# Attention ahead of two expert layers: 14 pieces of small diagonal tiles in place of 48 groups

## The chip, the cores and the metric

The kernel runs on one core of a Trainium2 chip. The metric is the time of one execution on the device in microseconds, median of three runs: 916.33 us (914.98 to 916.78) before. Of the core's engines, PE (TensorE) does matmuls and transposes and has a queue of its own for loading weights (PEld), DVE (VectorE) and POOL (GpSimd) do elementwise work and reductions, ACT (ScalarE) does functions and copies, SP issues the DMAs.

## The reference

q, k, v have shape (4 batches, 8 heads, 576 positions, 64). Heads 0 to 3 look back over a window of 32 positions, heads 4 to 7 at all earlier positions that lie a multiple of 32 back:

```python
scores = scale * np.matmul(q, k.transpose(0, 1, 3, 2))
rel = pos[:, None] - pos[None, :]
mask_local = (rel >= 0) & (rel < stride)                       # stride = 32
mask_strided = (rel >= 0) & (pos[None, :] % stride == pos[:, None] % stride)
scores = np.where(mask, scores, -1000000000.0)
attn = np.exp(scores - max); attn = attn / (sum + 1e-09)
x = attn @ v                                                   # -> x [2304, 512]
h = np.maximum(x @ w_in, 0.0);  x = h * h @ w_out              # d_ff 2048
h = x @ w_in2;  P = a0 + a1*h + a2*h**2 + a3*h**3
Q = 1 + abs(b0)*abs(h) + abs(b1)*h**2
out = (P / (Q + 1e-6)) @ w_out2
```

Everything is fp32; the weights reach the kernel as 64-bit doubles.

## The kernel before, in words

**Tokens and units.** The 2304 tokens are cut into 6 blocks of 384 (`NB`, `TB`), d_ff into 16 parts of 128 (`NF`). Step (j, f) of the first layer does `h_unit` (L473): 128 hidden rows for block j, 12 matmuls 128x384, since each fp32 product is made of three fp32r products (high by high, low by high, high by low). Two steps later `o_unit1` (L513) adds the squared, split hidden rows into four accumulators, 12 matmuls again. The second layer has the same `h_unit` and an `o_unit2` (L676) of nine matmuls 128x512. A "unit" is one of these: 384 in all. They run in order of j and f, block 0 first, and block j needs all heads of its 384 rows of `x`.

**Weights.** A half (`wraw`, 512 KB) comes from DRAM as int64, `to_f32` turns it into floats with one ACT operation (L210) and three DVE passes (L211, L212, L213), and `split_w` makes the high and low parts on POOL (L229, L230; the low part of the first four on DVE). The 32 halves of the first layer are converted by `feed_w` in the head and in block 0, two a step; those of the second layer in blocks 1 to 4, and go to a scratch in DRAM (`spill_w`). In block 0 the subtraction `gl` (L491) of the hidden rows' low part is on DVE too.

**Attention.** It is cut into 48 groups of one batch, one pair of heads and one third: a local group has two tiles of 96 queries by 128 keys for each head, a strided one all queries and keys of 14, 14 or 4 residue classes modulo 32, as tiles of 126x126 (seven classes of 18 positions) or 72x72 (four). Two groups share their loads and their scores: the two halves of the array's rows hold their 64-deep products. The mask is a matmul of an identity with a constant (L297) ahead of the scores (L305); from group 24 on it is added by DVE (L314). Then for each group: maximum (L317) and its product with -1/8 (L318) on DVE, one exponential on ACT for each tile and head with its sum read out behind it (L334), sum and reciprocal on DVE (L344, L345), product on POOL (L347), transposes on PE (L354), their copy out of PSUM (L360, L362), values on PE (L370), and `at_out`: the high part of `x` by ACT (L395), the low part by DVE (L396).

**Order.** Ahead of block 0 a loop over slots runs the groups that block 0 needs. The others are a list of pieces (a pair's scores with its softmax, or one group's values with another's transposes), and `paces` says how many of them must have been issued by each step; they stand ahead of the step's `h_unit`. PSUM has seven banks for everything ("ps") and one for weight bits.

The lines of the kernel before that the diff touches, and what calls them:

Of the kernel before, what the change touches and what calls it, by code (L numbers as in the profile page):

```python
# [9 lines left out]
F32 = mybir.dt.float32  # L10
# [8 lines left out]
P = 128  # L19
# [5 lines left out]
TB = 384  # L25
# [4 lines left out]
QL, KL = 96, 128  # L30
RG = ((0, 7), (14, 7), (28, 4))
MASKED = -8.0e9
C_L0, C_L1, C_S7, C_S4, C_ID, C_END = 0, 128, 256, 382, 454, 582


def _constants():

    c = np.zeros((P, C_END), np.float32)
    r, k = np.arange(QL)[:, None], np.arange(KL)[None, :]
    for at, rel in ((C_L0, r - k), (C_L1, r + STRIDE - k)):  # L40
        c[:QL, at : at + KL] = np.where((rel >= 0) & (rel < STRIDE), 0.0, MASKED)
# [8 lines left out]
class Group:


    def __init__(self, b, hp, i):
        self.b, self.hp, self.i = b, hp, i
        self.local = hp < NPAIR // 2
        if self.local:
            self.nt, self.nq, self.nk = 2, QL, KL
        else:  # L60
            self.r0, self.nr = RG[i]
            self.nt = 2 if self.nr == 7 else 1
            self.nq = self.nk = self.nr * NA
        self.name = f"{b}_{hp}_{i}"

    def q_positions(self):
        if self.local:
            return np.stack([np.arange(QL) + QL * (2 * self.i + t) for t in range(2)])
        a, r = np.arange(NA)[:, None], np.arange(self.nr)[None, :]
        return np.stack([(a * STRIDE + r + self.r0 + t * self.nr).ravel() for t in range(self.nt)])  # L70

    def k_positions(self):
        if self.local:
            return np.stack([np.arange(KL) + max(0, QL * (2 * self.i + t) - STRIDE) for t in range(2)])
        return self.q_positions()

    def k_starts(self):
        if self.local:
            return (0, 64) if self.i == 0 else (0, 96)
        return tuple(t * self.nk for t in range(self.nt))  # L80

    @property
    def qn(self):
        return self.nt * self.nq

    @property
    def kn(self):
        return 224 if self.local else self.qn

    def pieces(self):  # L90


        if self.local:
            t0 = self.b * S + 2 * QL * self.i
            return [(t0 // TB, t0 % TB, None)]
        out = []
        a = 0
        while a < NA:
            t0 = self.b * S + a * STRIDE
            n = min(NA - a, (TB - t0 % TB) // STRIDE)  # L100
            out.append((t0 // TB, t0 % TB, (a, n)))
            a += n
        return out


def _groups():

    out = []
    for b in range(B):
        strided = [Group(b, hp, i) for i in ((2, 0, 1) if b == 0 else range(3)) for hp in (2, 3)]  # L110
        local = {i: [Group(b, hp, i) for hp in (0, 1)] for i in range(3)}
        early = local[0] + local[1]
        out += early + strided + local[2] if b == 2 else strided + early + local[2]
    return out


def _last_group(groups):

    last = [0] * NB
    for n, g in enumerate(groups):  # L120
        for j, _, _ in g.pieces():
            last[j] = max(last[j], n)
    return last


QK_W = 1008
V_W = 2 * 2 * D


def _pack_qkv(q, k, v):  # L130

    groups = _groups()
    qk = np.zeros((len(groups), D, QK_W), np.float32)
    vp = np.zeros((len(groups) // 2, P, 2, V_W), np.float32)
    for n, g in enumerate(groups):
        h = slice(2 * g.hp, 2 * g.hp + 2)
        qpos = g.q_positions().ravel()
        if g.local:
            k0 = int(g.k_positions()[0, 0])
            kpos = np.arange(k0, k0 + g.kn) if k0 + g.kn <= S else np.arange(k0, S)  # L140
        else:
            kpos = qpos
        qk[n, :, : 2 * g.qn] = q[g.b, h][:, qpos].transpose(2, 0, 1).reshape(D, -1)
        kt = qk[n, :, 2 * g.qn : 2 * (g.qn + g.kn)].reshape(D, 2, g.kn)
        kt[:, :, : len(kpos)] = k[g.b, h][:, kpos].transpose(2, 0, 1)
        vt = v[g.b, h][:, g.k_positions()]
        vp[n // 2, : g.nk, n % 2, : g.nt * 2 * D] = vt.transpose(2, 1, 0, 3).reshape(g.nk, -1)
    return qk.reshape(len(groups) // 2, P, QK_W), vp.reshape(len(groups) // 2, P, 2 * V_W)
# [8 lines left out]
def moe_kernel(ctx, tc, qk, vp, w1, w2, a, b, masks, eye, out):  # L157
    nc = tc.nc
    groups = _groups()
    last = _last_group(groups)  # L160
    NG = len(groups)
# [17 lines left out]
    sms = [cpool.tile([P, 28], F32, name=f"sm{i}") for i in range(6)]  # L179
# [61 lines left out]
    st = {}  # L241
    loaded = [0]
    FIRST, PLACES, LATE, WARM = 12, 8, 24, 10

    def lags(n):

        return (3, 4) if n < FIRST else (2, 3)

    def load_qk(p):

        n = 2 * p
        if n >= NG:
            return
        g = groups[n]
        if n < FIRST:
            t = wpool.tile([P, QK_W], F32, tag=f"wh{NF - 1 - p}", name=f"qk{g.name}")
        else:
            t = apool.tile([P, QK_W], F32, tag="qk", name=f"qk{g.name}")
        w = 2 * (g.qn + g.kn)
        nc.sync.dma_start(t[:, :w], qk[p][:, :w])  # L260
        for m in range(2):
            st[n + m] = dict(qk=t[m * D : (m + 1) * D])

    def load_v(p):
        n = 2 * p
        if n >= NG:
            return
        g = groups[n]
        if n < FIRST:
            vt = wpool.tile([P, 2, 2, 2, D], F32, tag=f"w{'hl'[p % 2]}{7 - p // 2}", name=f"v{g.name}")  # L270
        else:
            vt = apool.tile([P, 2, 2, 2, D], F32, tag="v", name=f"v{g.name}")
        nc.sync.dma_start(vt, vp[p].rearrange("p (m t h d) -> p m t h d", m=2, h=2, d=D))
        for m in range(2):
            st[n + m]["v"] = vt[:, m]

# [491 lines left out]
```

## Time and profile before

| | us |
|---|---|
| median of three runs | 916.33 (914.98 to 916.78) |
| profiled execution, span | 912.5 |
| PE busy | 892.7 (98%) |
| DVE busy | 637.8 (70%) |
| POOL busy | 552.1 (61%) |
| ACT busy | 542.1 (59%) |

The span runs from the first to the last instruction of the profiled execution; the measured times also hold what lies around it, so the span stands 3.8 us below the median. Busy time is the time in which an engine has an instruction in work; PE's overlap in its pipeline, so that the durations of single matmuls in the timeline are longer than the distance from one start to the next. Small fp32 matmuls appear as two records each.

### The profile page before, as it was taken

What the parts mean: (1) busy time and instruction counts of PE and PEld (TensorE: products, weight loads), DVE (VectorE), ACT (ScalarE), POOL (GpSimd) and SP (SyncE); (2) the same over time, 40 slices, a digit from 0 to 9 for tenths busy, and PEclk for the clock granted to TensorE, in tenths of its full rate; (3) what the DMA queues carried; (4) which work ended last, traced back from release to release, by engine and by line L of the source; (5) the groups of instructions that cost most, each with busy time, mean ns of one, the idle gap of its engine ahead of it and who ended that gap; (6) DMA issues with size and microseconds to landing.
All of it is one profiled execution on the core that took longest, in us unless ns stands there. A gap on an engine that the chain in (4) does not pass through costs nothing.

```text
span 912.5 us, 14815 instructions
## 1 busy us (share of the span) xinstructions
PE 892.7 (98%) x5232; PEld 822.0 (90%) x5232; DVE 637.8 (70%) x888; ACT 542.1 (59%) x1384; POOL 552.1 (61%) x567
## 2 busy tenths in 40 slices
PE   7799899999999999999999999999999999999998
PEld 5589799998998999999999999989999999999896
DVE  5999865656465565554213598888888888888885
ACT  6777654445445554433325677776777767776763
POOL 2478755444454544544233496877787787777674
PEclk8899999999999999999999999999999999999999
DMA  8873445535544533532475710100100100100000
GB/s 325 284 233 122 124 132 159 167 111 169 174 138 141 181 129 118 167 109 77 162 263 214 250 38 1 54 18 1 52 18 1 53 18 1 44 1 1 36 0 35
DMA packets 40106, 98.56 MB, mean 108 GB/s; under 512 B 4704, under 2 KB 11616, under 8 KB 40032
## 3 DMA queue, kind: packets, MB, share of 16 engines
q1 hardware_dynamic: 40032, 97.62, 32.2%
q8 instruction: 41, 0.67, 0.3%
q14 instruction: 33, 0.27, 0.1%
HBM read 71.39 MB, written 26.21 MB: 107 GB/s over the span
## 4 chain that ended last, share of the span: by engine, by line
PE 84%; ACT 2%; DVE 1%; DMA 0%; issue 0%; POOL 0%; SPq 0%; ACTq 0%; POOLq 0%
PE h L473 40%; PE acc L676 22%; PE acc L513 18%; PE ps_t L354 1%; PE ps_v L370 1%; PE ps_s L305 1%; ACT e L334 1%; DMA x_scratch<-x 0%; DVE w L213 0%; DVE r L487 0%; DVE w L212 0%; DVE w L211 0%; ACT w L210 0%; ACT r L483 0%; POOL spl L230 0%
## 5 line engine op out<-in xcount | busy, mean ns | idle before, releaser
L473 PE MATMUL h<-xh,wh 128*128 128x384 f32 x768 | 263.2, 343 | 0.6 <-ACT e L334 0.6
L473 PE MATMUL h<-xh,wl 128*128 128x384 f32 x768 | 258.3, 336 | 0.0
L473 PE MATMUL h<-xl,wh 128*128 128x384 f32 x768 | 257.8, 336 | 0.0
L645 DVE RECIPROCAL h<-w 128x384 f32<-128x384 f32 x96 | 245.1, 2553 | 0.7 <-POOL w L642 0.7
L641 POOL TENSOR_TENSOR p<-p,hs 128x384 f32<-128x384 f32 x96 | 98.8, 1029 | 111.3 <-ACT p L639 111.3
L473 PEld LDWEIGHTS h<-xh,wh 128*128 128x128 f32 x768 | 144.7, 188 | 8.0 <-ACT e L334 1.8
L473 PEld LDWEIGHTS h<-xl,wh 128*128 128x128 f32 x768 | 144.8, 188 | 3.9
L473 PEld LDWEIGHTS h<-xh,wl 128*128 128x128 f32 x768 | 144.4, 188 | 0.0
L513 PE MATMUL acc<-gh,wh 128*128 128x384 f32 x384 | 129.0, 336 | 0.0
L513 PE MATMUL acc<-gh,wl 128*128 128x384 f32 x384 | 128.7, 335 | 0.0
L513 PE MATMUL acc<-gl,wh 128*128 128x384 f32 x384 | 128.6, 335 | 0.0
L491 POOL TENSOR_TENSOR gl<-r,gh 128x384 fp32r<-128x384 f32 x75 | 78.2, 1044 | 81.7 <-ACT gh L490 79.4
L483 ACT ACTIVATE r<-h 128x384 f32<-128x384 f32 x91 | 44.8, 492 | 119.7 <-PE h L473 113.0
L676 PE MATMUL acc<-wh,gl 128*128 128x512 f32 x288 | 113.9, 395 | 0.0
L676 PE MATMUL acc<-wl,gh 128*128 128x512 f32 x288 | 113.7, 395 | 0.0
L487 DVE TENSOR_TENSOR r<-r 128x384 f32<-128x384 f32 x75 | 55.9, 745 | 82.0 <-ACT r L483 81.6
L636 ACT ACTIVATE sq<-h 128x384 f32<-128x384 f32 x96 | 47.6, 496 | 110.0 <-PE h L473 106.5
L676 PE MATMUL acc<-wh,gh 128*128 128x512 f32 x288 | 111.9, 389 | 0.0
L643 DVE SCALAR_TENSOR_TENSOR p<-p,co,h 128x384 f32<-128x384 f32 x96 | 58.7, 612 | 65.6 <-POOL p L641 65.5
L662 POOL TENSOR_TENSOR gl<-rq,gh 128x384 fp32r<-128x384 f32 x96 | 99.1, 1033 | 2.0 <-ACT gh L661 2.0
L642 POOL TENSOR_TENSOR w<-w,sq 128x384 f32<-128x384 f32 x96 | 98.7, 1028 | 0.0
L490 ACT CAST gh<-r 128x384 fp32r<-128x384 f32 x91 | 47.1, 517 | 59.9 <-DVE r L487 59.5
(81 smaller groups left out, 1563.1 us busy)
## 6 DMA issues: line engine op xcount, KB each, us to landing
wraw<-in_w SPq DMA_DIRECT2D x64, 512.0 KB, 4.3
w_scratch<-sph SPq DMA_DIRECT2D x32, 256.0 KB, 4.2
w_scratch<-spl SPq DMA_DIRECT2D x32, 256.0 KB, 3.4
wh<-w_scratch SPq DMA_DIRECT2D x16, 512.0 KB, 3.6
wl<-w_scratch SPq DMA_DIRECT2D x16, 512.0 KB, 4.5
v<-in_vp SPq DMA_DIRECT2D x24, 256.0 KB, 3.9
qk<-in_qk SPq DMA_DIRECT2D x12, 416.0 KB, 3.8
x_scratch<-x SPq DMA_DIRECT2D x24, 192.0 KB, 2.5
```

Of the source, the lines that this page charges most:

```text
L473: nc.tensor.matmul(ps[:, :TB], w[:, c], x[:, kk, :], start=(kk == 0 and i == 0), stop=(kk == KT - 1 and i == 2))
L487: nc.vector.tensor_tensor(h, h, h, ALU.mult)
L490: last_act = nc.scalar.copy(gh, h).ins
L491: low = lambda: (nc.vector if psum_h or j == 0 else nc.gpsimd).tensor_tensor(gl, h, gh.bitcast(F32), ALU.subtract)
L513: nc.tensor.matmul(acc[j][e][:, :TB], w[:, c], g, start=(f == 0 and i == 0), stop=(f == NF - 1 and i == 2))
L636: keep(nc.scalar.activation(sq, h, AF.Square))
L641: keep(nc.gpsimd.tensor_tensor(p1, p1, hs, ALU.mult))
L642: keep(nc.gpsimd.tensor_tensor(w, w, sq, ALU.add))
L643: keep(nc.vector.scalar_tensor_tensor(p1, p1, a1, h, ALU.add, ALU.mult))
L645: keep(nc.vector.reciprocal(h, w))
L662: keep(nc.gpsimd.tensor_tensor(gl, rq, gh.bitcast(F32), ALU.subtract))
L676: nc.tensor.matmul(p, g[:, t * P : (t + 1) * P], w[:, c], start=(f == 0 and i == 0), stop=(f == NF - 1 and i == 2))
```

## The change

The 48 groups become 14 pieces. A strided piece is one batch and one pair of heads: 11 slots of three residue classes, each a tile of 54 queries by 54 keys (six slots in the upper half of the array's columns or rows, five in the lower, which overlap in one class). A local piece is one token block with all four local heads: 12 runs of 32 queries, each with the 64 keys that end with it. A piece's scores fill two PSUM banks, one for each head of the pair(s), 128 rows by 324 or 384 columns. Softmax is one chain a bank: maximum, subtraction into SBUF, one exponential of the whole bank on ACT, sum, 1e-9, reciprocal and POOL's product; then three 128x128 transposes, one copy, and values of 54 or 32 columns.

Of instructions, a strided piece has 24 score matmuls (64 deep, 64 rows, 54 columns), 6 transposes and 22 value matmuls, a local one 48 (64 deep, 32 rows, 64 columns), 6 and 48 (32 columns). Its loads are 585 KB and 384 KB, or 2 x 400 KB and 2 x 384 KB. Three pieces stand ahead of block 0; `PLAN` names the step of each other: scores and softmax ahead of that step's unit, both banks' transposes two steps on, values three steps on. The mask is a matmul up to piece 5 and a DVE addition from piece 6 on. The low part of all weights is on POOL, and the first eight weight halves are loaded right behind the loads of the head.

```diff
+    ORDER = [("s", 0, 2), ("s", 0, 3), ("l", 0), ("l", 1), ("s", 1, 2), ("s", 1, 3), ("l", 2), ("l", 3),
+             ("s", 2, 2), ("s", 2, 3), ("l", 4), ("s", 3, 2), ("s", 3, 3), ("l", 5)]
+    HEAD, MASK_PE = 3, 6
...
+    def at_scores(p):
+        for r in range(2):
+            p.ps[r] = psum.tile([P, 512], F32, tag="ps", name=f"ps_s{p.name}_{r}")
+        late = p.n >= MASK_PE
...
+            if not late:
+                pin(p, nc.tensor.matmul(to, cst[:, C_ID : C_ID + P], mask, start=True, stop=False, skip_group_check=True))
...
+        def score(r, at, col, lhs, rhs):
+            m = lhs.shape[1]
+            pin(p, nc.tensor.matmul(
+                p.ps[r][at : at + m, col * p.w : (col + 1) * p.w], lhs, rhs, start=late, stop=True, skip_group_check=True))
+
+        if p.strided:
+            t = p.qk[0]
+            for m in range(3):
+                for i in range(2):
+                    for s in range(2):
+                        u = min(2 * m + s, S_SLOTS[i][1] - 1)
+                        q0, k0 = (6 * i + u) * W3, QS_W + (S_SLOTS[i][0] + 3 * u) * NA
+                        for r in range(2):
+                            rows = slice(r * D, (r + 1) * D)
+                            score(r, s * 64, 2 * m + i, t[rows, q0 : q0 + 64], t[rows, k0 : k0 + W3])
+            return
+        for m in range(3):
+            for hp in range(2):
+                for c in range(4):
+                    j = 4 * m + c
+                    k0 = QL_W + _local_window(p.at, j)
+                    for r in range(2):
+                        x = p.qk[hp][r * D : (r + 1) * D]
+                        score(r, c * STRIDE, 2 * m + hp, x[:, j * STRIDE : (j + 1) * STRIDE], x[:, k0 : k0 + EW])
+
+    def at_softmax(p, r):
...
+        if p.n >= MASK_PE:
+            nc.vector.tensor_tensor(to, to, mask, ALU.add)
+        nc.vector.tensor_reduce(sm[:, 0:6], s3, AX.X, ALU.max)
...
+        nc.vector.tensor_tensor(ev, s3, wide(0), ALU.subtract)
+        nc.scalar.activation(ev, ev, AF.Exp, scale=1.0 / 8.0)
+        nc.vector.tensor_reduce(sm[:, 6:12], ev, AX.X, ALU.add)
+        nc.vector.tensor_scalar(sm[:, 12:18], sm[:, 6:12], 1e-9, None, ALU.add)
+        nc.vector.reciprocal(sm[:, 18:24], sm[:, 12:18])
+        nc.gpsimd.tensor_tensor(ev, ev, wide(18), ALU.mult)
...
+        for m in range(3):
+            src = p.e[r][:, 2 * m : 2 * m + 2, :].rearrange("p a k -> p (a k)")
+            pin(p, nc.tensor.transpose(ps[:, m * P : (m + 1) * P], src, ident))
...
+        nc.scalar.copy(p.t[r], ps[:, : 3 * P])
...
+        for j in range(12):
+            for i in range(2):
+                rows = slice(i * 64, (i + 1) * 64)
+                for r in range(2):
+                    value(i, r, j * STRIDE, STRIDE, p.t[r][rows, j * STRIDE : (j + 1) * STRIDE], p.v[r][rows, j, :])
...
-    while slot < last[0] + 5:
-        at_slot(slot)
...
+    at_scores(P0)
+    warm_up(2)
+    at_softmax(P0, 0)
+    at_softmax(P0, 1)
+    at_scores(P1)
+    at_softmax(P1, 0)
+    at_transpose(P0, 0)
+    at_softmax(P1, 1)
+    at_transpose(P0, 1)
+    at_scores(P2)
+    at_softmax(P2, 0)
+    at_values(P0)
+    at_softmax(P2, 1)
...
+    PLAN = {3: (0, 0), 4: (0, 5), 5: (0, 10), 6: (1, 1), 7: (1, 7), 8: (2, 0), 9: (2, 5), 10: (2, 10), 11: (3, 0), 12: (3, 5), 13: (3, 10)}
...
+        for step, do in ((0, sc), (2, tr_both), (3, va)):
+            at_unit.setdefault((j, f + step), []).append((do, pieces[n]))
```

On DVE, around the first two `gl` subtractions of block 0, before: `gl_0_0` and `gl_0_1` are those of the first two steps, L211 to L213 the three passes of a weight conversion, L317 a softmax maximum.

```order
L212 SCALAR_TENSOR_TENSOR bits_1_597<-wraw_1_1_302,bits_1_597 128x512
L491 TENSOR_TENSOR gl_0_0_633<-r_0_629,gh_0_0_632 128x384
L213 SCALAR_TENSOR_TENSOR wraw_1_1_302<-wraw_1_1_302,bits_1_597 128x512
L211 TENSOR_SCALAR bits_0_609<-w_0_4_0_608 128x512
L212 SCALAR_TENSOR_TENSOR bits_0_609<-wraw_4_0_370,bits_0_609 128x512
L491 TENSOR_TENSOR gl_0_1_689<-r_1_685,gh_0_1_688 128x384
L213 SCALAR_TENSOR_TENSOR wraw_4_0_370<-wraw_4_0_370,bits_0_609 128x512
L317 TENSOR_REDUCE sm_81<-ps_s_2_1_691 126x4
```

The same place after; the conversion's passes are L162 to L164 there, `gl` is L401, and L298, L308, L310 to L312 are the softmax of the local piece of block 1 (`sl`, `el`).

```order
L164 SCALAR_TENSOR_TENSOR wraw_2_0_119<-wraw_2_0_119,bits_0_480 128x512
L401 TENSOR_TENSOR gl_0_0_596<-r_0_592,gh_0_0_595 128x384
L401 TENSOR_TENSOR gl_0_1_638<-r_1_634,gh_0_1_637 128x384
L298 TENSOR_REDUCE sm_81<-ps_sl_0_487 128x6
L298 TENSOR_REDUCE sm_82<-ps_sl_1_488 128x6
L308 TENSOR_TENSOR el_0_540<-ps_sl_0_487,sm_81 128x384
L308 TENSOR_TENSOR el_1_548<-ps_sl_1_488,sm_82 128x384
L310 TENSOR_REDUCE sm_81<-el_0_540 128x6
L310 TENSOR_REDUCE sm_82<-el_1_548 128x6
L311 TENSOR_SCALAR sm_81<-sm_81 128x6
L162 TENSOR_SCALAR bits_1_560<-w_0_0_1_559 128x512
L312 RECIPROCAL sm_81<-sm_81 128x6
```

Before, conversions stand between the two subtractions and ahead of the next softmax; after, the subtractions and nearly the whole softmax of two banks stand ahead of the fourth conversion's first pass.

On PE, ahead of a step of block 2, before: values of one group and transposes of the next lie between an `acc` unit and an `h` unit.

```order
L513 MATMUL acc_2_3_2683<-gh_2_4_2780,wh_4_606 128x384
L513 MATMUL acc_2_3_2683<-gl_2_4_2781,wh_4_606 128x384
L513 MATMUL acc_2_3_2683<-gh_2_4_2780,wl_4_607 128x384
L370 MATMUL ps_v_2_1_2912<-at_2_1_2756,v_2_1_2567 64x126 x4
L354 MATMUL ps_t_3_1_2917<-ident,e_3_1_2637 126x126 x4
L473 MATMUL h_2_7_2928<-xh_2_797,wh_7_814 128x384
L473 MATMUL h_2_7_2928<-xl_2_798,wh_7_814 128x384
```

The same kind of place after, at step 2 of block 2: both banks of one piece are transposed, two steps behind its scores.

```order
L423 MATMUL acc_1_3_1810<-gh_1_15_2511,wh_15_1415 128x384
L423 MATMUL acc_1_3_1810<-gl_1_15_2512,wh_15_1415 128x384
L423 MATMUL acc_1_3_1810<-gh_1_15_2511,wl_15_1416 128x384
L320 MATMUL ps_ts_2_0_2664<-ident,es_2_0_2555 128x128 x3
L320 MATMUL ps_ts_2_1_2670<-ident,es_2_1_2565 128x128 x3
L383 MATMUL h_2_2_2676<-xh_2_1124,wh_2_477 128x384
L383 MATMUL h_2_2_2676<-xl_2_1125,wh_2_477 128x384
```

Values and transposes no longer share a visit; a visit holds the transposes of a whole piece.

## Rows read from the trace of the kernel before

**Rows 1.** The page: span, and each engine's busy time.
```profile
span 912.5 us, 14815 instructions
...
PE 892.7 (98%) x5232; PEld 822.0 (90%) x5232; DVE 637.8 (70%) x888; ACT 542.1 (59%) x1384; POOL 552.1 (61%) x567
```

**Rows 2.** The chain of waits: start us, us, what; one unit each.
```profile
348.46 2.08 PE acc L513 x12
...
525.98 2.08 PE acc L676 x9
```

**Rows 3.** Timeline of PE: start us, us, operation; first scores, two blocks' first, last matmul.
```profile
4.40 0.76 PE L305 MATMUL ps_s<-qk 64*72 64x72 f32 x8
...
41.61 0.42 PE L473 MATMUL h<-xh,wh 128*128 128x384 f32 x1
...
126.91 0.44 PE L473 MATMUL h<-xh,wh 128*128 128x384 f32 x1
...
908.34 0.39 PE L676 MATMUL acc<-wh,gl 128*128 128x512 f32 x1
```

**Rows 4.** Windows, head and block 0: length, PE, PEld, DVE, ACT, POOL busy, clock, DMA, GB/s.
```profile
0.00:41.60 41.60, 30.71 (x250) 20.50 (x251) 29.40 (x93) 27.54 (x130) 14.66 (x33) 0.84 0.88 317
41.60:126.90 85.30, 81.30 (x541) 74.30 (x539) 77.97 (x151) 55.84 (x162) 65.32 (x66) 0.98 0.52 164
```

**Rows 5.** Windows of the tiles ps_s, ps_t, ps_v: length, PE, PEld, DVE, ACT busy.
```profile
126.90:440.00 313.10, 12.34 (x178) 9.92 (x176) 27.83 (x50) 34.28 (x192) 1.00 0.43 138
...
126.90:440.00 313.10, 14.71 (x100) 9.39 (x100) 0.00 (x0) 13.17 (x27) 1.00 0.43 138
...
126.90:440.00 313.10, 15.42 (x208) 9.91 (x208) 11.70 (x40) 11.04 (x40) 1.00 0.43 138
```

**Rows 6.** Timeline of PE, block 3: two visits of the attention between units.
```profile
345.05 1.12 PE L305 MATMUL ps_s<-qk 64*96 64x128 f32 x16
346.09 0.44 PE L473 MATMUL h<-xh,wh 128*128 128x384 f32 x1
...
350.48 0.55 PE L370 MATMUL ps_v<-at,v 128*64 128x96 f32 x8
350.96 0.55 PE L354 MATMUL ps_t<-ident,e 96*128 96x96 f32 x4
351.29 0.42 PE L473 MATMUL h<-xh,wh 128*128 128x384 f32 x1
351.55 0.33 PE L473 MATMUL h<-xl,wh 128*128 128x384 f32 x1
```

**Rows 7.** Timeline of PE, block 0: small matmuls of 126 and 72 columns.
```profile
59.32 0.65 PE L370 MATMUL ps_v<-at,v 126*64 126x126 f32 x8
59.90 0.65 PE L354 MATMUL ps_t<-ident,e 126*126 126x126 f32 x4
60.31 0.42 PE L513 MATMUL acc<-gh,wh 128*128 128x384 f32 x1
...
64.78 0.48 PE L305 MATMUL ps_s<-qk 64*72 64x72 f32 x8
65.19 0.44 PE L473 MATMUL h<-xh,wh 128*128 128x384 f32 x1
```

**Rows 8.** Groups of instructions by shape: count, busy us, mean ns, idle before.
```profile
L211 DVE TENSOR_SCALAR bits<-w 128x512 int32<-128x512 int32 x32 | 22.0, 687 | 0.4 <-ACT w L210 0.2
L491 DVE TENSOR_TENSOR gl<-r,gh 128x384 fp32r<-128x384 f32 x16 | 15.0, 935 | 4.4 <-ACT gh L490 4.4
L347 POOL TENSOR_TENSOR e<-e,sm 126x504 f32<-126x504 f32 x12 | 12.4, 1030 | 17.5 <-DVE sm L345 17.5
L317 DVE TENSOR_REDUCE sm<-ps_s 126x4 f32<-126x504 f32 x16 | 10.3, 671 | 0.0
L396 DVE TENSOR_TENSOR xl<-ps_v,xh 128x192 fp32r<-128x192 f32 x24 | 8.4, 351 | 9.4 <-ACT xh L395 9.4
L318 DVE TENSOR_REDUCE sm<-sm 96x4 f32<-96x8 f32 x24 | 3.4, 149 | 0.0
```

More of the change, by code (lines that the diff above doesn't have):

```diff
@@ L47, in _constants @@
     c[:, C_ID : C_ID + P] = np.eye(P)
     return c.astype(mybir.dt.np(BF16)), np.eye(P, dtype=np.float32)
[L52 to L103, printed above, removed]
@@ L106, in _groups @@
-def _groups():
-    out = []
-    for b in range(B):
[L110 to L123, printed above, removed]
@@ L126 @@
[L126 to L148, printed above, removed]
+W3 = 54
@@ L378, in at_out @@
-    def at_out(n):
-        g, s = groups[n], st.pop(n)
-        ps = s["o"]
-        for j, t0, ar in g.pieces():
-            xh, xl = x_block(j)
-            if g.local:
-                views = [z[:, g.hp, t0 : t0 + 2 * QL] for z in (xh, xl)]
-                src = ps[:, : 2 * QL]
-            else:
-                a0, na = ar
+        for hp in range(2):
+            if p.n < HEAD:
+                t = wpool.tile([P, QKL_W], F32, tag=("wh7", "wl7")[hp], name=f"qk{p.name}_{hp}")
+            else:
+                t = apool.tile([P, QKL_W], F32, tag="qk", name=f"qk{p.name}_{hp}")
+            nc.sync.dma_start(t, ql[p.at, hp])
+            p.qk.append(t)
@@ new lines, in at_values, with value @@
+    def at_values(p):
+        p.o = [psum.tile([P, 512], F32, tag="ps", name=f"ps_v{p.name}_{i}") for i in range(2)]
+        def value(i, r, col, w, at, v):
+            pin(p, nc.tensor.matmul(
+                p.o[i][r * D : (r + 1) * D, col : col + w], v, at, start=True, stop=True, skip_group_check=True))
+        if p.strided:
+            for u in range(6):
+                for i in range(2):
+                    if u < S_SLOTS[i][1]:
+                        rows = slice(i * 64, i * 64 + W3)
+                        c0 = (u // 2) * P + (u % 2) * 64
+                        for r in range(2):
+                            value(i, r, u * W3, W3, p.t[r][rows, c0 : c0 + W3], p.v[0][rows, r, u, :])
+            return
+        for j in range(12):
+            for i in range(2):
+                rows = slice(i * 64, (i + 1) * 64)
+                for r in range(2):
+                    value(i, r, j * STRIDE, STRIDE, p.t[r][rows, j * STRIDE : (j + 1) * STRIDE], p.v[r][rows, j, :])
@@ new lines, in split_x, with at_out @@
+    def split_x(dst, src):
+        nc.scalar.copy(dst[0], src)
+        nc.vector.tensor_tensor(dst[1], src, dst[0].bitcast(F32), ALU.subtract)
+    def at_out(p):
+        if not p.strided:
+            x = x_block(p.at)
+            for hp in range(2):
+                split_x([z[:, hp, :] for z in x], p.o[hp][:, :TB])
+            return
+        a0 = 0
+        while a0 < NA:
+            t0 = p.at * S + a0 * STRIDE
+            na = min(NA - a0, (TB - t0 % TB) // STRIDE)
+            x = x_block(t0 // TB)
+            for i, (base, nu) in enumerate(S_SLOTS):
@@ L568, in load_raw @@
             place, free = homes[k]
-            if slot < free or place and any(homes[i][0] == place for i in range(done, k)):
+            if phase < free or place and any(homes[i][0] == place for i in range(done, k)):
                 break
@@ L708, in moe_kernel @@
         block0[0] = j == 0
[L709 to L714 removed]
+        for do, p in at_unit.get((j, f), ()):
+            do(p)
         while lows:
```

400 lines of the change are left out of this document (170 added, 230 removed).

## The prediction, made before the run

> **What bounds the kernel now.** I read the page first. TensorE (PE) is busy 892.7 of 912.5 us [rows 1], so time can only come from what PE does or from the few places where it stands still. The chain of waits says what its normal work costs: a unit, twelve 128x384 matmuls of `h` or `acc` or nine 128x512 ones of the second layer, takes 2.08 us wherever nothing else is mixed in [rows 2]. There are 6 blocks x 16 steps x 4 products = 384 units, 798.7 us, which this change leaves alone. So 912.5 - 798.7 = 113.8 us is all that it can touch.
>
> The timeline of PE says where those lie. The first `h` starts at 41.61, that of block 1 at 126.91, the last matmul at 908.34 [rows 3]; 4.1 us follow it. Block 0 holds 16 `h` and 14 `acc` units (62.4 us) in its 85.3 us: 22.9 us are over. From 126.91 on, 384 - 30 = 354 units are left, 736.3 us of 781.4; 45.1 us are over. Head 41.6, block 0 22.9, stream 45.1, tail 4.1: together 113.7.
>
> The windows tell head and block 0 apart [rows 4]. In the head PE is busy 30.7 of 41.6 us with the softmax chains of some ten groups between its bursts. In block 0 VectorE (DVE) is the fuller engine against what it has to do: 77.97 of 85.30, with weight conversion, the `gl` subtractions and softmax. Later PE runs without gaps, and the attention costs what its bursts add to PE.
>
> **Part 1, the head.** Before, the first block of `h` waits for ten groups; now for three pieces (`s0_2`, `s0_3`, `l0`). Scores of before started at 4.40 on a load of 144 KB, 128 x 288 floats [rows 3]. The first load is now 585 KB and stands with a 142 KB mask ahead of the first softmax; 583 KB more at the 317 GB/s of the head [rows 4] is 1.9 us, so I put the first score at about 6.3 and the first bank at 6.6. All loads of the head, 3.8 MB, need 12 us at that rate: the first weights land near 16, ahead of their turn on DVE.
>
> Then DVE's order decides, since it has to pass these before `x` of block 0 is whole: three wide passes (maximum, subtraction, sum) for each of six banks. A wide pass over 126x504 takes 0.671 us [rows 8], so 0.43 for 324 columns and 0.51 for 384: 4 banks x 3 x 0.43 + 2 x 3 x 0.51 = 8.2. Twelve small ones at the 0.149 of the 4-column reduction [rows 8]: 1.8. `xl` at 0.351 for 192 columns [rows 8]: 594 columns for each strided piece, 768 for the local one, 1956 in all: 3.6. Two weight conversions of three passes of 0.687 [rows 8]: 4.1. The sum is 17.7, and 6.6 + 17.7 = 24.3. Instructions start a little before the one ahead has ended, which takes perhaps 1 off; exponentials, POOL products and transposes that DVE waits for put 1 to 6 on. I take first `h` at 25, with 22 to 31 as its ends.
>
> **Part 2, block 0.** An earlier start is not all kept, because the conversions were spread over head and block 0 and now nearly all fall into block 0. DVE has from the third to the 29th conversion, 27 x 2.06 = 55.6; 14 `gl` subtractions x 0.935 = 13.1 [rows 8]; the local piece `l1` 6 x 0.51 + 4 x 0.15 + 1.4 = 5.1; two strided pieces 2 x (6 x 0.43 + 0.6 + 1.1) = 8.6: together 82.4. PE has 62.4 of units and some 9 of attention, 71.5, so DVE binds. The two fences of the change show an early loss: DVE now comes to two `gl` and both softmax banks of `l1` before conversion four goes on, and the transposes of `l1` stand in PE's order ahead of the third `h`. For that idle time of DVE, and for the split on POOL behind the last conversion, I add 4.6. Block 0 takes 87, 25 + 87 = 112 for `h` of block 1 (107 to 118), against 126.91: 15 us gained.
>
> **Part 3, the stream.** Before, from 126.9 on the attention's bursts are busy 12.34, 14.71 and 15.42 us, 42.5 together [rows 5]. They lie in 40 visits between units. A burst's busy time runs some 0.08 beyond where the next starts (345.05 + 1.12 against 346.09; 350.48 + 0.55 against 350.96; at a transpose 0.22), and the first `h` behind it starts 0.1 slower than its fellows [rows 6]. So about 0.1 of each visit is counted twice, and 42.5 - 4 = 38.5 is what goes.
>
> After it come eight pieces (four strided, four local), each with three visits. The prices: four pairs of values took 0.58 at 126 columns, four pairs of scores 0.41 at 72 [rows 7], that is 0.17 / 4 / 54 = 0.79 ns a column and pair, and 0.18 for the start. A pair at 54 columns is then 0.045, at 64 0.052, at 32 0.027. Two records make one fp32 matmul; the two row or column halves run as a pair. Transposes: four in 0.41 [rows 7], so six 0.65, with their start 0.86. Three visits start for 0.3 each, 0.9.
> How many small tiles run beside each other, four or eight, is shown by no row, so I bound it.
> - From below, all that differ in place run together. Strided: 12 x 0.045 + 11 x 0.045 = 1.0; local: 12 x 0.052 + 24 x 0.027 = 1.3. With 1.76 for the rest, 4 x (2.8 + 3.1) = 24.
> - Two at a time, as in the rows: strided 24 x 0.045 + 22 x 0.045 = 2.1; local 48 x 0.052 + 48 x 0.027 = 3.8. 4 x (3.9 + 5.6) = 38.
> - None beside another: twice that without the rest, 4 x (5.9 + 9.4) = 61.
>
> I take 31, midway between the first two, since the nearest rows show pairs and nothing shows a limit at two. So the stream changes by 31 - 38.5 = -7.5.
> The Trainium skill, "TensorE: Matmul & The Clock Gate", section "Wait — 56ns, not 53.3ns?", says that matmuls never start closer than about 25 ns apart however few columns they have. By that, an estimate from its figure: 4 x (92 + 192) x 0.025 + 14 = 42 in place of 31, and a time about 11 us later. No row here goes below it: 72 columns have (0.41 - 0.18) / 8 = 28 ns a record [rows 7]. It is rival 1 below, with the row's own figure.
>
> **Part 4, a wait that is added.** Transposes of both banks stand two units of work (8.3 us of PE) behind their scores. What has to fit: add, maximum, subtraction, sum on DVE for two banks, 8 x 0.5 = 4, exponentials, one POOL product a bank (1.03 at 504 columns [rows 8], so 0.7 to 0.8), and a conversion of 2.06 that may stand between on DVE. That is 6 to 9 us. Behind a transpose that waits, PE's `h` and all of the following stand still. Nine to eleven pieces times 0 to 1 us: I take 2 in the stream (0 to 8).
> Costs that I put at nothing: the mask add of late pieces (two of some 0.5 on DVE, which is busy 78 us of 85 only in block 0; late pieces come after it), ACT's one exponential in place of four, POOL's memsets, the loads of later pieces, issued a whole piece ahead of their use. If DVE's cover goes, they count as part of the 8.
>
> **Sum.** 112 + 781.4 - 7.5 + 2 = 887.9 for the last matmul, against 908.34; with the 4.1 of the tail a span of 892. The profiled execution's span, 912.5, lies 3.8 us below the median of 916.33, which I add: 896.
>
> **Rivals.**
> 1. *The number of small matmuls binds.* A record costs 28 ns however many run beside each other: strided 92 x 0.028 = 2.6, local 192 x 0.028 = 5.4, with 1.76 each 4 x (4.3 + 7.1) = 46, 15 more than taken, and 2 in head and block 0: 913. For it: nothing in the trace is faster per record. Against it: what limits the pairs there is their columns, since the price goes with them.
> 2. *The head's gain is lost in block 0.* PE waits at each of the three pieces for the softmax that stands behind conversions on DVE (rows of DVE's order), 3 x 3 us more, and the head ends near 27: `h` of block 1 at 121, 905. For it: DVE is 77.97 of 85.30 full already [rows 4]. Against it: fewer groups are left to do there.
> 3. *Slower: small tiles run one after another.* If a change of place in the array drains what is in flight, the stream's bursts cost 61 in place of 31, and head and block 0 lose 6: 932. It decides from A = 51 on, where the gain of the other parts is used up. For it: nothing shows more than two beside each other; against it: the pairs do overlap, 0.58 for eight at 126 columns, which is 0.07 a record [rows 7], when one alone by the same 0.79 ns would be 0.1.
> The Trainium skill, "TensorEngine Tiling (Array Packing)", section "Instruction Overhead", speaks for the dearer end too: each matmul has some 60 cycles of overhead, one column costs as much as sixty, and a dimension that is already small should not be tiled. An estimate by it: local values at 32 columns would cost like 60, about 1 us more for each local piece, 900 in all.
>
> **How the numbers follow.** Forecast 896 with 0.60: its own range is 884 to 906 (head and block 0 from 107 to 118, bursts from 24 to 38). Rival 1 0.15, rival 2 0.16, rival 3 0.09. The range for 8 in 10 reaches over rivals 1 and 2: 882 to 917; left out are rival 3, the far side of rival 1 and a little below. This kernel's runs differ by 0.2% (914.98 to 916.78 around 916.33), so less than that is no change. Faster: 0.60 + 0.16 and 0.07 of rival 1 = 0.83. Same: 0.04 of rival 1. Slower: 0.09 and 0.04 of rival 1 = 0.13.
>
> **What would show it.** First `h` between 22 and 31; `h` of block 1 between 107 and 118 with DVE over 90% busy between them; the local score bursts under 2.7 us, and local value bursts under 1.4 (between 1.3 and 2.7 for rival 1, more for rival 3); waits of PE on POOL's product or ACT's copy before transposes and values under 8 us in all. A first `h` past 35, or bursts at twice the two-at-a-time price, would make the prediction wrong.

## The result, and the profile after

The changed kernel takes 893.23 us (median of 892.89 to 893.34) against 916.40; the ratio is 0.9758, 95% interval 0.9733 to 0.9783. The forecast was 896. Its total is closer than its terms, and that is luck: block 0 came out 4.7 us longer and the stream 6.7 us shorter than forecast, and the two errors nearly cancel.

The page of the changed kernel, against [rows 1]: PE has 27.5 us less and DVE 13 less; DVE is still the fullest of the three helper engines in the first slices.

```profile
span 891.1 us, 16392 instructions
...
PE 865.2 (97%) x6312; PEld 807.2 (91%) x6312; DVE 624.5 (70%) x791; ACT 486.4 (55%) x1017; POOL 535.0 (60%) x555
```

The timeline of PE at the places of [rows 3]: first `h`, first `h` of block 1 (the burst from 115.24 to 118.2 holds the twelve matmuls of step 15 and three of block 1, interleaved; by count block 1 begins with the one at 117.70), last matmul.

```profile
25.96 0.66 PE L383 MATMUL h<-xh,wh 128*128 128x384 f32 x1
...
117.70 0.33 PE L383 MATMUL h<-xl,wh 128*128 128x384 f32 x1
...
886.95 0.39 PE L608 MATMUL acc<-wh,gl 128*128 128x512 f32 x1
```

| stretch | before | forecast | after |
|---|---|---|---|
| head, to the first `h` | 41.6 | 25 | 26.0 |
| block 0, to block 1's first `h` | 85.3 | 87 | 91.7 |
| stream, to the last matmul | 781.4 | 775.9 | 769.2 |
| tail | 4.1 | 4.1 | 4.1 |
| span | 912.5 | 892 | 891.1 |

The two rows in the middle do not hold the same units. Between the two first `h`, PE has 168 records of `acc` before, which is 14 units, but only 156 after, which is 13: one unit of 2.08 us has passed from block 0 into the stream. With it in its old place block 0 takes 93.8 and the stream 767.2, so that the two terms were off by 6.8 and 8.7.

The windows of head and block 0 (columns as in [rows 4]): block 0 has about the DVE load that was forecast (79.2 us, 82.4 forecast), but takes 91.7 us to carry it, with a granted clock of 0.93 where it was 0.98.

```profile
0.00:26.00 26.00, 18.31 (x411) 12.40 (x411) 15.81 (x47) 10.83 (x27) 8.32 (x18) 0.79 0.95 355
26.00:117.70 91.70, 78.85 (x748) 71.44 (x748) 79.20 (x143) 47.08 (x97) 61.51 (x67) 0.93 0.52 183
```

Windows of the stream for the attention's tiles, scores strided and local, transposes strided and local, values strided and local (PE busy first): 25.7 us together, where [rows 5] add up to 42.5.

```profile
117.70:430.00 312.30, 3.68 (x192) 3.17 (x192) 10.01 (x24) 1.00 0.46 153
...
117.70:430.00 312.30, 4.68 (x384) 4.04 (x384) 11.51 (x24) 1.00 0.46 153
...
117.70:430.00 312.30, 3.76 (x24) 2.75 (x24) 3.65 (x8) 1.00 0.46 153
...
117.70:430.00 312.30, 3.54 (x24) 2.77 (x24) 3.40 (x8) 1.00 0.46 153
...
117.70:430.00 312.30, 3.62 (x176) 3.11 (x176) 4.69 (x16) 4.13 (x16) 1.00 0.46 153
...
117.70:430.00 312.30, 6.41 (x384) 5.96 (x384) 4.08 (x8) 3.45 (x8) 1.00 0.46 153
```

Single bursts of the stream in PE's timeline, against [rows 6, 7]: from a burst's start to the `h` behind it, 96 records of local scores take 1.10 us, 96 of local values 1.53, 48 of strided scores 0.85.

```profile
124.03 1.17 PE L269 MATMUL ps_sl<-qkl 64*32 64x64 f32 x96
125.13 0.44 PE L383 MATMUL h<-xh,wh 128*128 128x384 f32 x1
...
139.33 1.60 PE L330 MATMUL ps_vl<-atl,vl 64*64 64x32 f32 x96
140.86 0.45 PE L383 MATMUL h<-xh,wh 128*128 128x384 f32 x1
...
219.20 0.92 PE L269 MATMUL ps_ss<-qks 64*64 64x54 f32 x48
220.05 0.44 PE L383 MATMUL h<-xh,wh 128*128 128x384 f32 x1
```

The early loss of block 0 in DVE's timeline: the two `gl` and the softmax of `l1` stand ahead of the next conversion (L162). Between 28.9 and 37.4 us DVE does 4.1 us of work.

```profile
28.24 0.69 DVE L164 SCALAR_TENSOR_TENSOR wraw<-wraw,bits 128x512 int32<-128x512 int32 x1
31.41 0.56 DVE L401 TENSOR_TENSOR gl<-r,gh 128x384 fp32r<-128x384 f32 x1 [2.48 <-ACT gh L400]
33.78 0.56 DVE L401 TENSOR_TENSOR gl<-r,gh 128x384 fp32r<-128x384 f32 x1 [1.81 <-ACT gh L400]
34.26 1.01 DVE L298 TENSOR_REDUCE sm<-ps_sl 128x6 f32<-128x384 f32 x2
...
37.35 0.69 DVE L162 TENSOR_SCALAR bits<-w 128x512 int32<-128x512 int32 x1
```

In block 0 as a whole DVE waits for ACT's `gh` at its `gl` subtractions (us in total, times, longest), twice the 4.4 us of before [rows 8]:

```profile
DVE gl L401 <- ACT gh L400: 8.7, 6, 2.5
```

PE's timeline behind that softmax: the transposes of `l1` stand ahead of the third `h` and wait 6.07 us for POOL's product.

```profile
39.16 1.69 PE L320 MATMUL ps_tl<-ident,el 128*128 128x128 f32 x6 [6.07 <-POOL el L313]
```

From block 1 on PE hardly waits; these are all its waits between 117.6 and 350 us:

```profile
PE ps_tl L320 <- POOL el L313: 0.4, 2, 0.2
PE ps_ts L320 <- POOL es L313: 0.4, 1, 0.4
PE h L383 <- ACT r L393: 0.4, 1, 0.4
PE h L383 <- DVE xl L350: 0.2, 1, 0.2
```

### The profile page after: what moved, and what is told of

It is laid out like the page before. It is cut to its first block, busy times and chain, and to the rows that moved or that the text cites. A ratio compares the mean times of both kernels' runs of the same rounds, so it can differ in the third digit from the quotient of the medians.

```text
span 891.1 us, 16392 instructions
## 1 busy us (share of the span) xinstructions
PE 865.2 (97%) x6312; PEld 807.2 (91%) x6312; DVE 624.5 (70%) x791; ACT 486.4 (55%) x1017; POOL 535.0 (60%) x555
## 4 chain that ended last, share of the span: by engine, by line
PE 86%; DVE 5%; DMA 3%; ACT 2%; POOL 2%; issue 1%; SPq 0%; POOLq 0%; DVEq 0%; ACTq 0%
PE h L383 42%; PE acc L608 22%; PE acc L423 18%; PE ps_vl L330 1%; DMA qks<-in_qs 1%; DMA qkl<-in_ql 1%; PE ps_vs L330 1%; PE ps_tl L320 1%; DVE r L397 1%; POOL wl L181 1%; PE ps_sl L269 1%; DVE sm L298 1%; ACT w L161 1%; DVE w L164 1%; DVE sm L310 1%
## 5 line engine op out<-in xcount | busy, mean ns | idle before, releaser
L401 POOL TENSOR_TENSOR gl<-r,gh 128x384 fp32r<-128x384 f32 x75 | 76.8, 1025 | 117.3 <-ACT gh L400 115.2
```

The lines of the kernel that those rows point to most:

```text
L401: low = lambda: (nc.vector if psum_h or j == 0 else nc.gpsimd).tensor_tensor(gl, h, gh.bitcast(F32), ALU.subtract)
```

## The experiments

Two questions were open: how small tiles share the array (the stream came out 6.7 us cheaper), and what holds block 0 (4.7 us dearer). Times are compared by stretch, since the first `h` lies between 25.9 and 27.5 in runs whose head is the same up to small edits. It goes with the scores of the second piece: where they start at 7.0 to 7.1 us, as in the changed kernel, the first `h` stands at 25.9 to 26.5; where they start at 8.4 to 8.7, at 27.1 to 27.5. Why they start late in some runs is open.

**1. The later pieces, later.**

```diff
-    PLAN = {3: (0, 0), 4: (0, 5), 5: (0, 10), ...
+    PLAN = {3: (0, 3), 4: (0, 7), 5: (0, 11), ...
```

> The three pieces that stand inside block 0 move: their scores from steps 0, 5 and 10 to steps 3, 7 and 11. Theory (the supply of converted weight halves by DVE binds block 0, and DVE's 8 us of idle between 26 and 37 us are lost for good): DVE goes on with conversions there, block 1 starts at 111 in place of 117.7, time 887. Rival A (PE's own work and the transfers bind block 0): block 1 stays within 2 us of 117.7, time 891 to 895. Rival B (the later pieces now hold up block 1's start): slower than 895.

891.71 us, ratio 0.9732 (0.9715 to 0.9749). The stall of 6 us is gone, and block 0 takes 88.2 in place of 91.7: half of what was expected, as DVE still waits 7.4 us for ACT's `gh` inside its order. By its marks (block 1 at 115.7, 891.71 us) this is the outcome of rival A, so by its time alone DVE could be the bound or not. The window of block 0, columns as before:

```profile
27.50:115.70 88.20, 79.34 (x748) 70.42 (x749) 78.08 (x141) 45.77 (x95) 60.26 (x65) 0.97 0.54 182
```

PE's waits in block 0 stand now at the weights' parts alone, 9.5 us in all; the two largest are shown. POOL makes these parts, and stands idle in its turn for 17.7 us between 26 and 117 behind DVE's conversions.

```profile
PE acc L423 <- POOL wl L181: 4.0, 7, 1.3
PE h L383 <- POOL wl L181: 2.8, 6, 0.7
```

**2. Two places at a time.** `walk` is the list of a burst's matmuls, in the order of issue. For scores, m, i and hp name columns of the bank, s or c is the place in the array's columns and r the half of its rows; for values, u or j names columns, i is the half of the rows and r that of the columns.

```diff
+            walk = [(m, hp, c, r) for m in range(3) for hp in range(2) for c in range(4) for r in range(2)]
+            if p.n >= MASK_PE:
+                walk.sort(key=lambda z: z[2])      # likewise s of strided scores, i of values
```

> In the eight pieces after block 0 the small matmuls are issued place by place in the array, so that only the two row halves (scores) or column halves (values) alternate; the work is the same. Theory (up to eight tiles in different places run beside each other, and two at a time cost 0.79 ns a column and pair): local scores 1.10 -> 2.7 us, strided scores 0.8 -> 1.3, strided values 0.84 -> 1.2, local values unchanged at 1.5: 9.5 us more, 903. Rival (the rate of issue sets the price, whatever the place): 893, all bursts as they are.

905.38 us, ratio 0.9889 (0.9865 to 0.9913); the stream takes 780.5, 11.3 more. Scores came near what was expected (local 2.24 for 2.7, strided 1.35 for 1.3), and so did strided values (1.24 to 1.45 for 1.2). Local values did not: the four bursts take 2.71 to 2.94 where the price by columns gave 1.5. PE's timeline, with the dearest of the four:

```profile
125.65 2.31 PE L269 MATMUL ps_sl<-qkl 64*32 64x64 f32 x96
127.89 0.44 PE L389 MATMUL h<-xh,wh 128*128 128x384 f32 x1
...
141.24 3.01 PE L332 MATMUL ps_vl<-atl,vl 64*64 64x32 f32 x96
144.18 0.44 PE L389 MATMUL h<-xh,wh 128*128 128x384 f32 x1
```

**3. One place at a time.**

```diff
-                walk.sort(key=lambda z: z[2])
+                walk.sort(key=lambda z: (z[2], z[3]))   # half outermost too
```

> As the run before, but all matmuls of one place come in a row, so that none stands beside another. Theory: local scores 96 x 0.052 = 5.0, strided scores 2.2, strided values 2.0, local values 2.6 us, together 4 x (11.8 - 4.3) = 30 us more, 923. Rival (issue rate): 893. If changes of place drained the array, this would be the cheaper order: under 890.

935.12 us, ratio 1.0209 (1.0188 to 1.0230): slower than before the change. The stream takes 811.5, 42.3 more. So the order of the same instructions is worth 42 us, and the gain of the stream hangs on neighbours in PE's queue that differ in place. PE's timeline, with the dearest burst of local values; the four take 6.67, 5.09, 5.09 and 6.45:

```profile
125.80 4.19 PE L269 MATMUL ps_sl<-qkl 64*32 64x64 f32 x96
129.92 0.44 PE L389 MATMUL h<-xh,wh 128*128 128x384 f32 x1
...
143.27 6.74 PE L332 MATMUL ps_vl<-atl,vl 64*64 64x32 f32 x96
149.94 0.69 PE L389 MATMUL h<-xh,wh 128*128 128x384 f32 x1
```

The two dear bursts are dear by the clock. Windows of the burst at 143.27 and of the `h` behind it (columns as in [rows 4]): the granted clock falls inside the burst and is 0.50, the lower of the two levels (1.2 of 2.4 GHz), behind it. PE had been busy all the time, with small matmuls in one place.

```profile
143.27:145.50 2.23, 2.23 (x43) 2.23 (x42) 0.00 (x0) 0.35 (x1) 2.15 (x3) 1.00 0.74 245
145.50:149.94 4.44, 4.44 (x58) 4.38 (x56) 0.56 (x1) 0.48 (x1) 0.35 (x1) 0.60 0.51 166
149.94:152.00 2.06, 2.06 (x7) 2.06 (x7) 0.56 (x1) 0.48 (x1) 0.00 (x0) 0.50 0.67 187
```

The bursts of 5.09 run at a clock of 1.00. At that clock the order costs, by an estimate from the single bursts, 4 x (3.02 for local scores + 3.56 for local values + 1.52 for strided scores + 1.30 for strided values) = 38 of the 42 us.

**4. Local values with 64 columns.**

```diff
-                    value(i, r, j * STRIDE, STRIDE, ...
+                    w = STRIDE * (2 if p.n >= MASK_PE and j < 11 else 1)
+                    value(i, r, j * STRIDE, w, ...
```

> The local value matmuls of the four late pieces have 64 columns in place of 32 (the second half is written again by the next one), as many instructions. Theory (96 records in 1.5 us is a limit by the number of records, about 15 ns each, since four places at 32 columns need 0.65): four at a time at 64 columns need 1.25, so the burst stays at 1.5 to 1.7 and the time at 893 to 894. Rival (two at a time, columns set the price): 48 x 0.052 + 0.2 = 2.7 us a burst, 898.

892.73 us, ratio 0.9745 (0.9721 to 0.9769), and the burst takes 1.53 as before. In four places the number of records sets its price, not the columns. PE's timeline:

```profile
139.53 1.60 PE L330 MATMUL ps_vl<-atl,vl 64*64 64x64 f32 x96
141.06 0.45 PE L384 MATMUL h<-xh,wh 128*128 128x384 f32 x1
```

**5. Block 0's low parts on POOL.** With the edit of run 1.

```diff
-        low = lambda: (nc.vector if psum_h or j == 0 else nc.gpsimd).tensor_tensor(gl, h, ...
+        low = lambda: (nc.vector if psum_h else nc.gpsimd).tensor_tensor(gl, h, ...
-        if n % 4 == 0 and n > 2 * NF:
+        if (n % 4 == 0 and n > 2 * NF) or (n % 2 == 0 and 3 < n <= 2 * NF):
             nc.scalar.copy(wh, wf)
```

> On top of the first run (pieces at steps 3, 7 and 11) the low parts of block 0's hidden rows go from DVE to POOL, and every second high part of a weight half in block 0 from POOL to ACT. Theory (DVE's in-order stream binds block 0: 81 us busy of 88 and 7.4 us of waiting for ACT inside it, all at these subtractions): DVE loses 14 x 0.6 us of work and the waits, POOL has 62.5 + 16.5 - 8.6 = 70 us; block 0 goes from 88.2 to about 80, the time to 883 to 885. Rival (POOL, with its in-order waits for ACT, takes DVE's place): block 0 stays at 86 or more, 890 or slower.

906.98 us, ratio 0.9899 (0.9881 to 0.9917): block 0 takes 101.1, as the rival said and by far. The waits (us in total, times, longest) say why: POOL now stands in its order behind ACT for 25.8 us, with the weight splits queued behind it, ACT behind DVE's conversions for its copies, and DVE for ACT's first step of the conversion.

```profile
POOL gl L401 <- ACT gh L400: 25.8, 13, 2.7
ACT r L393 <- PE h L383: 19.3, 13, 4.7
DVE bits L162 <- ACT w L161: 19.0, 12, 4.4
...
ACT wh L178 <- DVE wraw L164: 11.4, 5, 2.8
```

This tests a move of work and a new coupling at once, so it says nothing on DVE's load.

**6. All masks on DVE.** `HEAD, MASK_PE = 3, 0` in place of `3, 6`.

> All masks are added by DVE, those of the first six pieces too (12 additions of about 0.45 us, 6 of them ahead of block 0, 6 inside it); PE loses 12 mask matmuls of some 0.2 to 0.4. Theory (DVE binds head and block 0): 2.7 us later start, 2 to 3 us longer block 0, 897 to 899. Rival (PE binds there): 3 us shorter, 890. Rival (both have slack): 893.

896.01 us, ratio 0.9778 (0.9763 to 0.9794). The first `h` stays at 26.0; block 0 goes from 91.7 to 95.3. In block 0 six additions, 3.0 us of DVE, cost 3.6; they also stand in the chain of the softmax that PE's transposes wait for, so the cost need not be DVE's load alone. In the head nothing was lost, perhaps because the mask matmuls that PE no longer does stood in the same chain.

**7. Six exponentials a bank.**

```diff
-        nc.scalar.activation(ev, ev, AF.Exp, scale=1.0 / 8.0)
+        for c in range(6):
+            nc.scalar.activation(ev[:, c], ev[:, c], AF.Exp, scale=1.0 / 8.0)
```

> Six exponentials of 54 or 64 columns a bank in place of one of 324 or 384, each some 0.3 us by the 72-column form of before, so 1.8 in place of 0.5 a bank. Theory (the head is one chain of DVE and ACT, the stream has cover): first h 3 to 6 us later, block 0 0 to 2 us longer, nothing after it: 896 to 901. Rival (ACT's work is covered everywhere): 893 to 894. Rival (the two steps between scores and transposes in the stream are used up): each of eight visits waits 1 us more, above 903.

897.17 us, ratio 0.9792 (0.9777 to 0.9807): first `h` 28.3, block 0 93.4 (1.7 more), stream 769.0 (none). One exponential a bank is worth 3.9 us, all of it before block 1. The first `h` is 2.3 later than in the changed kernel, but the second piece starts late here too, at 8.79; against the runs in which it does (27.1 to 27.5), 0.8 to 1.2 us are the exponentials' own.

**8. All masks on PE.** `HEAD, MASK_PE = 3, 14`.

> All masks are matmuls, those of the eight late pieces too: 16 more mask matmuls on PE, 0.43 us for two, and 16 DVE additions of 0.45 less. Theory (PE binds after block 0, DVE's part is covered): 8 x 0.43 = 3.5 us slower, 896 to 897. Rival (PE waits there for the chain behind the mask): up to 1 us faster than that for each visit, 889 to 893.

894.78 us, ratio 0.9767 (0.9752 to 0.9782). The stream takes 770.2, 1.0 more, where eight pairs of masks at 0.43 would be 3.4. The time lies between the two theories: some of PE's price comes back, and which of the waits gives it was not settled.

**9. Two passes for a weight half, the first left out.** With the edit of run 1.

```diff
-        nc.vector.tensor_scalar(bits, w, 3, 0x7FFFFFFF, ALU.logical_shift_left, ALU.bitwise_and)
+        if layer: nc.vector.tensor_scalar(bits, w, 3, 0x7FFFFFFF, ALU.logical_shift_left, ALU.bitwise_and)
-        nc.vector.scalar_tensor_tensor(bits, hi, -0x80000000, bits, ALU.bitwise_and, ALU.bitwise_or)
+        nc.vector.scalar_tensor_tensor(bits, hi, -0x80000000, bits if layer else w, ALU.bitwise_and, ALU.bitwise_or)
```

> The first run (pieces at steps 3, 7 and 11) with two DVE passes in place of three for each weight half of the first layer: the shift by three and its mask are left out, so the first layer's weights are wrong; everything else runs as before. Theory (DVE's throughput binds block 0): some 28 passes of 0.69 less, block 0 from 88.2 us to what PE needs, 74 to 78, time 878 to 882. Rival (the order of waits DVE to POOL to PE to ACT binds, not DVE's load): block 0 at 84 or more, 888 or slower.

889.58 us, ratio 0.9719 (0.9703 to 0.9734): block 0 stays at 90.0, as the rival said (87.9 with the 13 `acc` units of run 1; here, as in run 12, it holds 14). But DVE is as busy as in run 1, 80.4 us with 25 instructions fewer. The window of block 0:

```profile
27.10:117.10 90.00, 79.65 (x761) 75.62 (x762) 80.42 (x116) 47.17 (x99) 75.64 (x70) 0.91 0.56 194
```

The groups of DVE's instructions from 26 to 117 us (mean ns behind the comma) show why: the pass that now reads both operands from SBUF takes 1126 ns where it was 689 in run 1, the `gl` subtractions 1096 where they were 807.

```profile
L164 DVE SCALAR_TENSOR_TENSOR bits<-wraw,w 128x512 int32<-128x512 int32 x29 | 32.7, 1126 | 2.0 <-ACT w L161 0.4
...
L402 DVE TENSOR_TENSOR gl<-r,gh 128x384 fp32r<-128x384 f32 x16 | 17.5, 1096 | 3.0 <-ACT gh L401 3.0
```

POOL's busy time rises too, from 60.3 to 75.6. So the run did not take away the load that it was made to take away.

**10. Fillers in the head.** `warm_up(8)` behind the second piece's scores, `warm_up(2)` behind the first transposes, `warm_up(5)` behind the second piece's.

> The changed kernel with 15 more filler matmuls (128x512 bf16) in PE's waits of the head: eight behind the second piece's scores, two behind the first transpose, five behind the second piece's transposes. Theory (from 12 us on the granted clock is 0.5 to 0.8, and so the values of 1.90 us, the transposes of 1.69, the local values of 2.78 and the first h of 3.4 each take 0.8 to 1.3 longer than at full clock): they run at full clock, first h 3 us earlier, 890. Rival (the clock stays low all the same, or the fillers delay the chain): 893 to 896.

889.86 us, ratio 0.9720 (0.9702 to 0.9738), but for another reason than expected in this profile: the clock from 12 to 20 us is 1.00 in place of 0.64 and 0.78, the strided values take 1.29 in place of 1.90, while the local values (2.49 for 2.78) and the first `h` (0.50 from start to start) stay slow, and the first `h` starts at 25.8. That is only 0.2 earlier than in the changed kernel, but the second piece starts at 8.56 here; the runs without fillers in which it starts so late have their first `h` at 27.1 to 27.5, so the fillers give some 1.4 to 1.8 us. That profiled execution took 891.88, the three others 889.41 to 889.97, so the rest of the gain is not explained by this trace. PE's timeline:

```profile
18.83 1.29 PE L330 MATMUL ps_vs<-eas,vs 54*64 54x54 f32 x44 [0.61 <-ACT eas L324]
...
22.64 2.49 PE L330 MATMUL ps_vl<-eal,vl 64*64 64x32 f32 x94 [0.34 <-ACT eal L324]
```

**11. Runs 1 and 10 together.**

> The first run and the fillers together. Theory (independent gains): 888 to 889. Rival (an earlier start is lost in block 0, where DVE binds): 891.5 as the first run alone.

889.30 us, ratio 0.9716 (0.9701 to 0.9732): first `h` 25.6, block 0 87.5. It is the fastest of those that leave nothing out, and below the rival's 891.5, but no different from run 10 within the intervals.

**12. Two passes for a weight half, the second left out.** With the edit of run 1.

```diff
-        nc.vector.scalar_tensor_tensor(bits, hi, -0x80000000, bits, ALU.bitwise_and, ALU.bitwise_or)
+        if layer: nc.vector.scalar_tensor_tensor(bits, hi, -0x80000000, bits, ALU.bitwise_and, ALU.bitwise_or)
```

> As the run with two passes for each weight half, but the pass that is left out is the second, which sets the sign, so the first layer's weights are all positive; the first pass still writes to PSUM, so no pass reads its two operands from SBUF (there the run before had 1126 ns for a pass in place of 689, and 1096 in place of 807 for the subtractions, so that DVE's load had hardly fallen). Theory (DVE's throughput binds block 0): 28 x 0.69 = 19 us of DVE gone, block 0 from 88.2 to 74 to 79 us, time 878 to 883. Rival (POOL's two passes of 2.0 us for each half and the chain of waits around them bind): block 0 at 84 or more, 887 or slower.

877.05 us, ratio 0.9576 (0.9560 to 0.9592). Here DVE's load does fall, to 63.6 us, and block 0 goes from 88.2 to 77.9, with PE busy 75.6 of it. With 13 `acc` units as in run 1 it would be 75.8, 12.4 less. The window of block 0:

```profile
25.90:103.80 77.90, 75.64 (x761) 72.81 (x762) 63.55 (x116) 47.12 (x99) 65.78 (x69) 0.96 0.67 236
```

PE's waits for the weights' parts fall from the 9.5 us of run 1 to this one; 2.2 us more are spent ahead of a burst of scores, for DVE's `xl`:

```profile
PE h L384 <- POOL wh L181: 0.6, 1, 0.6
```

## Why the prediction held, step by step

**Head: the time right, the mechanism in part.** 25 was forecast, 26.0 came. The forecast let DVE's order decide; DVE is busy 15.8 of the 26.0 us, and the time is one chain of DVE, ACT, POOL and PE. Run 7 shows that ACT's exponential lies on it. What the forecast did not have is PE's clock. The granted clock is 0.64 from 12 to 16 us, after a stretch (8 to 12) in which PE was busy 0.58 of 4 us, and 0.50, the lower level, from 20 to 26, where PE is busy 5.78 of 6 us; before, it was 0.50 from 12 to 16, 0.97 from 20 to 26 and 0.74 from 26 to 33. At the lower level the last strided values take 1.86 us from their start to the next, in place of 0.84 in the stream.

**Block 0: the mechanism right, a term mis-sized.** That DVE's passes bind it is shown by run 12: 14.5 us less of DVE gave 10.3 (12.4 with the same units), and then PE's load is the bound; run 6 fits (3.0 us more cost 3.6). DVE's sum was put at 82.4 and is 79.2. The failed term is the 4.6 "for that idle time of DVE, and for the split on POOL": DVE stands idle 12.5 us in block 0, 8.7 of them at `gl` subtractions that wait for ACT's `gh`. So the sum of load and loss was put at 87.0 and is 91.7. The order had been read, but the loss was not worked out: `gl` in DVE's order waits for `h`, and the conversion that the next `h` needs stands behind it. Run 1 removes the piece of it that the plan makes, 3.5 us. PE's clock is a second candidate that was not separated: it is 0.82, 0.70 and 0.77 in the stretches 26 to 33, 33 to 39 and 39 to 46 us and 0.77 from 67.7 to 75, else 1.00, and in run 1, with the shorter block 0, it is 0.97 on average.

**Stream: the sign right, the price mis-sized.** The bursts were taken at 31, midway between all places beside each other (24) and two at a time (38). The stream after holds 355 units, 738.4 us. With the same 6.6 us of other time as before, 769.2 - 738.4 - 6.6 = 24.2 is what they and their waits cost, so the lower bound. Runs 2 and 3 show the overlap that no row of before could: 96 local score records take 1.10 us in eight places, 2.24 in two, 4.12 in one. The 2 us of added wait came to 1.4 at most, all that PE waits between 117.6 and 350 us.

**What is not in the columns.** The price of 0.79 ns a column and pair came near for scores in two places (2.24 against 2.7, 1.35 against 1.3), not for local values: 1.53 at 32 and at 64 columns (run 4), and 2.71 to 2.94 in two places, where the columns gave 1.48. Counted by place, a record of local values costs nearly the same in four, two and one: 1.53 / 24 = 64 ns, 2.71 / 48 = 56, 5.09 / 96 = 53 (at full clock), so the places run beside each other. For local scores that ends before eight places: 1.10 / 12 = 92 ns there, 47 in two, 43 in one. The floor was the number of records, as rival 1 had it, but at 11 to 19 ns a record over all places and not at 28, so it costs (1.53 - 0.83) x 4 = 2.8 us at the local values, where it was put at 15 in all.
The Trainium skill, "TensorE: Matmul & The Clock Gate", section "Wait — 56ns, not 53.3ns?", gives about 25 ns as the least from start to start, and the estimate from it was 42 for the bursts. The trace differs: 1.10 / 96 = 11.5 ns a record in eight places and 16 to 19 in four, and only two places or one (23 to 53 ns at full clock) come to about 25 or above. The Trainium skill, "TensorEngine Tiling (Array Packing)", section "Instruction Overhead", lets a matmul of one column take as long as one of 60; run 4 agrees in kind, with 1.53 us at 32 and at 64 columns.

**Rivals.** Rival 2 (waits in block 0) is in the result with half of its price or more, 4.7 of 9, or 6.8 with the same units. Rival 3 is refuted, since the order with the fewest changes of place is the dearest (run 3); that its 935.12 lies near the rival's 932 is chance. The time around the span was put at 3.8 us and is 1.8 for the profiled execution (892.89). By its own bounds (block 1 at 118, bursts at 38) the top of the range adds up to 909, not to 906; the "A" of rival 3 is the cost of the bursts.

**Signs.** The first `h`, block 1's start and the local scores came as named. Three signs did not: DVE is busy 86% of block 0 (79.20 of 91.70) and not over 90; local values take 1.53 us, above 1.4 and inside what was named for rival 1; and PE waits 8.3 us for POOL's product before transposes in block 0 alone, where under 8 were named for all. They point at the two terms that were mis-sized.

## What to carry to other kernels

When work is cut into tiles smaller than the array, the order in which places alternate in PE's queue is part of the design: here it was worth 42 us, some 38 of them, by the estimate above, at full clock. When a head is shortened, list for each helper engine what now falls into the first block, and look in its order for instructions that wait on the block's own results; their waits, more than the sum of their work, were missing here. And an experiment that takes work off an engine has to be read by that engine's busy time first: run 9 left it unchanged.

## What the runs showed of the hardware that was not expected

**DVE beside POOL.** A `gl` subtraction, both operands in SBUF, takes 0.56 us while POOL is idle (the one at 31.41, shown above; POOL's rows end at 31.14 and begin again at 38.27) and 1.64 while POOL splits weights from 45.19 on. DVE's timeline of the changed kernel:

```profile
45.27 1.64 DVE L401 TENSOR_TENSOR gl<-r,gh 128x384 fp32r<-128x384 f32 x1 [0.47 <-ACT gh L400]
```

POOL's timeline at the second:

```profile
45.19 1.30 POOL L181 TENSOR_TENSOR wl<-wraw,wh 128x512 fp32r<-128x512 f32 x1
```

In these rows the one that starts first goes first: the `gl` at 56.86 takes 0.56 again, and the split on POOL that starts behind it, at 56.94, takes 1.65 in place of 1.3.

The Trainium skill, "SBUF — State Buffer", section "Who interferes with whom", says that a DVE instruction with two SBUF inputs contends with a POOL instruction that reads SBUF, and one with at most one, outside the two-port modes, does not. Run 9 (1126 against 689 ns) agrees, and would be a reason to keep a conversion's bits in PSUM, as this kernel does.

**One place in a row.** At full clock local values at 32 columns take 5.09 / 96 = 53 ns a record, strided ones at 54 columns 2.14 / 44 = 49, local scores at 64 columns 43. So the columns hardly set the price in one place either; what sets it was not tried. The 6.67 us of the burst shown in run 3 (69 ns a record) are those of a clock that fell inside it.
